# Blocks of 32 columns in place of 64 for the one-hot products of a gated mixing kernel

## The chip, the cores and the metric

The kernel runs on one core of one Trainium2 chip. The metric is the device time of one execution in microseconds; the time of a kernel is the median of its runs. The engines are TensorE (PE in the profile, its weight loads PEld), VectorE (DVE), ScalarE (ACT), GpSimd (POOL) and SyncE (SP), which here only issues transfers.

## What is computed

Two branches read the same input x of 2048 tokens by 640, and a sigmoid gate mixes them. Branch A is a Fourier mixing layer in real arithmetic. Branch B routes each token, for each of 32 heads, to two of 256 = 16 x 16 experts.

```python
a = x @ dft_hid_re.T;  b = x @ dft_hid_im.T
A = dft_seq_re @ a - dft_seq_im @ b
s1, s2 = scores of q1 with k1 and of q2 with k2      # 16 each, per token and head
# the two best of each, the two best of their four sums: expert = e1 * 16 + e2
g = softmax(the two best sums)
B = sum over heads and the two: g * gelu(x . u[expert]) * v[expert]
g0 = sigmoid(sum(x * gate_w))
out = g0 * A + (1 - g0) * B
```

For branch B the kernel never gathers rows of u and v. It computes gelu(x . u) for all 256 experts and multiplies it by a dense weight of each token and expert: the sum of the gates of the (head, choice) pairs that picked this expert. That dense weight, 16 x 16 a token, is what the changed lines compute.

## The kernel before

The order of all work is written out in the program, engine by engine; nothing is reordered later. The main loop goes over 128 sequence pieces (`seq_piece`, 4 column blocks of 512 x 16 pieces x 2 matrices). Each piece is 15 products (5 blocks of 128 by `mm3`, lines 143 to 145, three products each, since fp32 values are split in a high and a low part). Pieces are loaded five ahead (`load_piece`), and split on ScalarE and GpSimd three ahead. Behind the 128 pieces come 2 x 42 last steps (`step`), which multiply by the hidden transform and by v.

Between the products, `run_bg` lets a planner (`Pump`) put in work of branch B: every three products give it 0.68 us x 0.95 of credit, and each piece of background work, a generator, yields what it is charged. The order in which VectorE gets its work, and where TensorE turns aside for branch B, follows from these charges alone.

The scores, the two best, and the gates are made first. A transpose by DMA then gives `ROWS`, in which a partition is one (head, choice) pair (128 of them) and the columns are tokens: the first index, the second index (both as powers of two) and the gate. `experts` goes through 32 sets of 64 tokens. For each:

- `build` (line 836) makes on VectorE two tables of 128 x 1024 fp16 (lines 844 and 845): `pt` and `qt`, which hold for token and expert half e a one where the pair picked e; `pt` is then multiplied by the gate. Their columns are ordered (m, e, t): 16 groups m of four tokens t, and inside a group 16 halves e of four tokens each.
- `use` (line 848) multiplies them on TensorE, up to three sets in one visit. The sum over the 128 pairs is the contraction. One product takes the 64 columns of `pt` of one group (four tokens) as weights and the 64 columns of `qt` as the moving operand. The result is 64 x 64 for (e, t) by (f, t'); only the sixteenths with t = t' are wanted, in all a quarter. Two such blocks lie side by side in the 128 partitions of a PSUM bank.
- `mask` (line 812) clears what is not wanted: four ScalarE activations, each over the columns of one t', with a scale by partition (`mask4`) that is zero except where t = t'.
- `add_up` (line 817) sums the four columns of t' on VectorE and puts the result into `cd`, so that a partition is (block, e, t).
- `settle` (line 826) calls mask and add_up for one set each and charges 0.75 us; it runs ahead of each of the three table operations of a later set.

`store_gates` (line 793) writes `cd`, half by half, to DRAM in the order (token, e, f, m); `load_z` reads it much later for the last steps. Banks 6, 7 and 5 hold the three sets of a visit. The mask table comes from the identity matrix once (lines 342, 357 and 358). Line 380 (`w_part`) is another narrow product that the prediction compares with: 32-column weights in four blocks of partitions.

Of the kernel before, what the change touches and what calls it, by code (L numbers as in the profile page):

```python
# [8 lines left out]
F32 = mybir.dt.float32  # L9
# [3 lines left out]
AF = mybir.ActivationFunctionType  # L13
OP = mybir.AluOpType
AX = mybir.AxisListType
PSUM = bass.MemoryType.PSUM

P = 128
# [3 lines left out]
E = 16  # L22
# [12 lines left out]
GSCALE = 32768.0  # L35
# [71 lines left out]
def gated_mix_kernel(ctx: ExitStack, tc: tile.TileContext, xT, xn, dreT, dimT, wsre, wsim, wq, kT, uT, vv, gw, out):  # L107
    nc = tc.nc
    ctx.enter_context(tc.manual_schedule())

    const = ctx.enter_context(tc.tile_pool(name="const", bufs=1))
# [10 lines left out]
    def bank(n, shape=(P, TC), dt=F32):  # L122
        return psum.tile(list(shape), dt, name=f"b{n}", tag=f"b{n}")
# [4 lines left out]
    def ps_t(shape, dt=F32):  # L128
        return bank(7, shape, dt)
# [20 lines left out]
    gd = [dram.tile([2, 4, E, E, P], F32, name=f"gd{g}", tag=f"gd{g}") for g in range(2)]  # L150
# [98 lines left out]
    for q in range(2 * NC):  # L249
        n = NT * (q + 1)  # L250
# [72 lines left out]
    t = ps_t([P, TC])  # L323
    for n in range(WARM):
        c = slice(0, 2 * P) if n < WARM - 1 else slice(2 * P, TC)
# [12 lines left out]
    identf = p1.tile([P, P], F32, name="identf", tag="uf", bufs=2)  # L338
    wtab4 = const.tile([P, E, 4], F16)
    powers = const.tile([P, E], F16)  # L340
    top_bits = const.tile([P, 1], F32)
    mask4 = const.tile([P, 4], F32)

    def put_keys():
        for r in range(2):
# [6 lines left out]
    def make_tables():  # L352
        for e in range(E):
            nc.gpsimd.memset(powers[:, e:e + 1], 2.0 ** (E - 1 - e))
        nc.gpsimd.memset(top_bits, INF)
        nc.gpsimd.tensor_copy(wtab4, powers[:, :, None].to_broadcast([P, E, 4]))
        nc.vector.tensor_reduce(mask4, identf.rearrange("p (a b) -> p b a", b=4), op=OP.add, axis=AX.X)
        nc.vector.tensor_scalar(mask4, mask4, 1.0 / GSCALE, None, op0=OP.mult)

    for n, f in ((2, put_keys), (4, make_ident), (9, make_tables)):  # L360
        at(n, f)
# [124 lines left out]
    for G in range(NG):  # L486
        b = 6 + 3 * G
# [9 lines left out]
    n = b + 2  # L497
# [275 lines left out]
    for p in range(NP):  # L773
        n = N0 + 4 * p + min((p + 1) // 2, 3)
# [3 lines left out]
    for n in range(2 * NT + 3, 4 * NT + 3):  # L778
        s = n % NT
# [11 lines left out]
    summed, stored = {}, set()  # L791

    def store_gates(g):
        if g in summed and g not in stored:
            for s in range(2):
                nc.sync.dma_start(gd[g][s].rearrange("t e f m -> e t f m"), summed[g][64 * s:64 * s + 64])
            stored.add(g)

    free_sets = deque(range(4))
    HOT, used = [], []  # L800

    def experts():


        shp = [P, 16, E, 4]
        wt = wtab4[:, None].to_broadcast(shp)
        todo = deque((g, c) for g in range(2) for c in range(16))
        cd = {}

        masked, unmasked = deque(), deque()  # L810

        def mask(t):
            f = t.rearrange("p m (e t) -> p (m e) t", t=4)
            for n in range(4):
                nc.scalar.activation(f[:, :, n], f[:, :, n], AF.Copy, scale=mask4[:, n:n + 1])  # L815

        def add_up(g, c, t):
            if c == 0:
                store_gates(g - 1)
                cd[g] = p3.tile([P, E, P], F32, name="cd", tag="cd")  # L820
            nc.vector.tensor_reduce(cd[g][:, :, 8 * c:8 * c + 8].rearrange("p e m -> p m e"),
                                    t.rearrange("p m (e t) -> p m e t", e=E), op=OP.add, axis=AX.X)
            if c == 15:
                summed[g] = cd[g]

        def settle(force=False):
            us = 0.0
            if masked:
                add_up(*masked.popleft())
                us = 0.75  # L830
            if unmasked and (force or not closing):
                masked.append(unmasked.popleft())
                mask(masked[-1][2])
            return us

        def build(g, c, s):
            pt, qt = (HOT[s // 2][:, s % 2, n].rearrange("p (m e t) -> p m e t", e=E, t=4) for n in range(2))

            def row(n):
                r = ROWS[g][:, n, 8 * c:8 * c + 8, :].rearrange("p b (s t) -> p (b s) t", t=4)  # L840
                return r[:, :, None, :].to_broadcast(shp)

            assert rowed >= set(range(8 * g, 8 * g + 8))
            for o, a, b, op in ((pt, row(0), wt, OP.is_equal), (qt, row(1), wt, OP.is_equal), (pt, pt, row(2), OP.mult)):
                nc.vector.tensor_tensor(o, a, b, op=op)  # L845
                yield (0.8 if early else 1.05) + settle()

        def use(group):
            assert not last_part
            while masked or unmasked:  # L850
                yield settle(True)
            for i, (g, c, s) in enumerate(group):
                t = bank((6, 7, 5)[i], (P, 8, E * 4))
                pt, qt = (HOT[s // 2][:, s % 2, n].rearrange("p (m c) -> p m c", m=16) for n in range(2))
                for m in range(16):
                    r = slice(64 * (m % 2), 64 * (m % 2) + 64)
                    nc.tensor.matmul(t[r, m // 2, :], pt[:, m], qt[:, m], start=True, stop=True)  # L857
                unmasked.append((g, c, t))
                used.append((g, c))
                free_sets.append(s)  # L860
            yield 0.0 if todo else 4.0

        prev = []
        while todo or prev:
            group = []
            while todo and len(group) < (2 if ending else 3):
                free = [s for s in free_sets if s < 2 or not ending]
                if prev and (not free or ending and any(s > 1 for g, c, s in prev)):
                    yield from use(prev)
                    prev = []  # L870
                    continue
                if not free:
                    break
                s = min(free) if ending else free[0]
                free_sets.remove(s)
                g, c = todo.popleft()
                group.append((g, c, s))
                yield from build(g, c, s)
            if prev:
                if not group:  # L880
                    yield 2.2
                yield from use(prev)
            prev = group
        while masked or unmasked:
            yield settle(True)
# [103 lines left out]
    at(NPC - 3, make_sums, KD)  # L989
    at(NPC + 3, split_sums, KD)  # L990
    at(NPC + 14, store_gates, 1)


# [55 lines left out]
    for k, (n, m) in enumerate(((-1, 2), (0, 4), (5, 7), (7, 9), (10, 12))):  # L1049
        n, m = NT * (NC + 2) + n, NT * (NC + 2) + m  # L1050
# [19 lines left out]
    def load_z(b, n):  # L1070

        c = 2 * b + n
        bg.drain(lambda: b in summed)
        store_gates(b)
        nc.sync.dma_start(take((b, "g", n)), gdr[S + c * TC:S + (c + 1) * TC].partition_broadcast(P))
        for k in range(2):
            a, f = take((b, f"a{n + 1}{k + 1}", KD)), take((b, "zf", 2 * n + k))
            nc.sync.dma_start(a, actd[k][:, c * TC:(c + 1) * TC])
            nc.sync.dma_start(f.rearrange("p (t m) -> p t m", t=4),
                              gd[b][n].rearrange("t e f m -> (e f) t m")[k * P:(k + 1) * P])  # L1080
# [223 lines left out]
```

## Time and profile before

| | us |
|---|---|
| median of three runs | 750.85 |
| lowest and highest run | 750.09, 751.49 |
| span of the profiled execution (its total is not given apart) | 748.7 |
| TensorE matmul busy | 743.8 (99%) |
| TensorE weight loads busy | 603.8 (81%) |
| VectorE busy | 585.7 (78%) |
| ScalarE busy | 365.9 (49%) |
| GpSimd busy | 342.4 (46%) |

The span runs from the first to the last instruction of the program; the runs' time also has what lies around it. Busy time of an engine is the union of its instructions. Matmuls overlap one another, so the distance from one start to the next, not the duration, tells what one of them takes of TensorE.

### The profile page before, as it was taken

How to read it: one execution, taken by the hardware profiler on the slowest of the kernel's cores; microseconds unless marked ns; L12 is line 12 of the kernel's file. 1: busy time of each engine (PE TensorE's matmuls, PEld its weight loads, DVE VectorE, ACT ScalarE, POOL GpSimd, SP SyncE). 2: the span in 40 equal slices, each digit the busy share in tenths (PEclk: the TensorE clock that was granted, in tenths of full speed). 3: DMA queues.
4: the chain of work that ended last, by engine and by line, in shares of the span. 5: the costliest groups of instructions: out<-in, count | busy, mean ns of one | idle time of the engine just before them, and what ended most of it. 6: DMA issues, size and time to landing. Idle time of an engine off the chain costs nothing.

```text
span 748.7 us, 11141 instructions
## 1 busy us (share of the span) xinstructions
PE 743.8 (99%) x3925; PEld 603.8 (81%) x3925; DVE 585.7 (78%) x741; ACT 365.9 (49%) x664; POOL 342.4 (46%) x286
## 2 busy tenths in 40 slices
PE   9999999999999999999999999999999999999998
PEld 7777767888888888888888888888888888888887
DVE  6964098495999899999999888979899974357651
ACT  4325234543544745555463686633545653443451
POOL 5533325440532424145235456643455793487253
PEclk9999999999999999999999999999999999999999
DMA  9999999777556786972398766488876689775301
GB/s 333 392 380 364 344 374 354 231 222 250 129 176 141 190 242 157 237 200 79 114 395 285 162 168 188 133 255 280 266 234 197 222 262 343 219 239 172 113 29 71
DMA packets 84488, 171.11 MB, mean 229 GB/s; under 512 B 16080, under 2 KB 21328, under 8 KB 84176
## 3 DMA queue, kind: packets, MB, share of 16 engines
q1 hardware_dynamic: 70960, 146.13, 57.9%
q0 software_dynamic: 5472, 9.96, 8.5%
q10 hardware_dynamic: 8000, 14.31, 5.2%
q8 instruction: 31, 0.51, 0.3%
q14 instruction: 25, 0.20, 0.1%
HBM read 136.40 MB, written 32.39 MB: 225 GB/s over the span
## 4 chain that ended last, share of the span: by engine, by line
PE 94%; DMA 5%; SPq 0%; DVE 0%; ACT 0%; issue 0%; ACTq 0%
PE b L143 30%; PE b L145 30%; PE b L144 30%; PE b L239 2%; DMA wf<-in_wsre 2%; PE b L380 2%; DMA wq<-in_wq 1%; PE b L857 1%; DMA xd<-X 1%; DMA gdr<-gc 1%; DVE wp L386 0%; SPq L177 0%; ACT WS L295 0%; ACTq L514 0%; DVE ST L1191 0%
## 5 line engine op out<-in xcount | busy, mean ns | idle before, releaser
L143 PE MATMUL b<-WS,X 128*128 128x512 f32 x620 | 243.3, 392 | 0.0
L144 PE MATMUL b<-WS,X 128*128 128x512 f32 x620 | 241.4, 389 | 0.0
L145 PE MATMUL b<-WS,X 128*128 128x512 f32 x620 | 241.3, 389 | 0.0
L139 POOL TENSOR_TENSOR WS<-wf,WS 128x512 fp32r<-128x512 f32 x89 | 131.9, 1486 | 168.3 <-ACT WS L138 151.8
L143 PEld LDWEIGHTS b<-WS,X 128*128 128x128 f32 x620 | 116.3, 188 | 28.2 <-issue 4.1
L145 PEld LDWEIGHTS b<-WS,X 128*128 128x128 f32 x620 | 116.4, 188 | 24.4
L144 PEld LDWEIGHTS b<-WS,X 128*128 128x128 f32 x620 | 116.4, 188 | 23.6
L138 ACT ACTIVATE WS<-wf 128x512 fp32r<-128x512 f32 x89 | 55.5, 626 | 69.0 <-PE b L145 40.9
L845 DVE TENSOR_TENSOR hot<-rows,wtab 128x1024 f16<-128x1024 f16 x64 | 57.8, 930 | 4.3 <-PE b L857 4.3
L139 POOL TENSOR_TENSOR xl<-xf,xh 128x640 fp32r<-128x640 f32 x16 | 27.2, 1702 | 72.0 <-ACT xh L138 72.0
L567 ACT ACTIVATE sc<-b 128x512 f32<-128x512 f32 x32 | 19.9, 621 | 80.8 <-PE b L145 77.0
L191 POOL DMA_DIRECT2D WS<-in_wsre x30 | 26.4, 881 | 61.8 <-ACT WS L189 60.5
L139 POOL TENSOR_TENSOR WS<-ra,WS 128x512 fp32r<-128x512 f32 x33 | 47.1, 1439 | 14.3 <-ACT WS L138 14.1
L815 ACT ACTIVATE b<-b,mask 128x128 f32<-128x128 f32 x128 | 43.1, 342 | 14.9 <-PE b L857 11.8
L138 ACT ACTIVATE WS<-ra 128x512 fp32r<-128x512 f32 x47 | 29.4, 631 | 42.4 <-PE b L145 29.6
L622 DVE TENSOR_TENSOR eq<-sc,mm 128x1024 f16<-128x1024 f32 x32 | 44.4, 1387 | 0.9
L629 DVE TENSOR_REDUCE tied<-eq 128x64 f32<-128x1024 f16 x32 | 39.0, 1219 | 0.9
L620 DVE TENSOR_REDUCE mm<-sc 128x64 f32<-128x1024 f32 x32 | 38.7, 1211 | 0.2
L139 POOL TENSOR_TENSOR WP<-ra,WP 128x512 fp32r<-128x512 f32 x13 | 19.2, 1490 | 31.0 <-ACT WP L138 30.9
L217 DVE SCALAR_TENSOR_TENSOR ST<-ST,grow 128x512 f32<-128x512 f32 x40 | 31.7, 855 | 1.7 <-ACT tw L138 1.7
L845 DVE TENSOR_TENSOR hot<-hot,rows 128x1024 f16<-128x1024 f16 x32 | 31.6, 986 | 0.0
L143 PE MATMUL b<-WU,xh 128*128 128x512 f32 x80 | 31.1, 389 | 0.0
(209 smaller groups left out, 1449.1 us busy)
## 6 DMA issues: line engine op xcount, KB each, us to landing
X<-xd SPq DMA_DIRECT2D x36, 640.0 KB, 6.5
wq<-in_wq SPq DMA_DIRECT2D x32, 640.0 KB, 7.1
wf<-in_wsim SPq DMA_DIRECT2D x64, 256.0 KB, 4.8
wf<-in_wsre SPq DMA_DIRECT2D x63, 256.0 KB, 6.4
ra<-pd SPq DMA_DIRECT2D x40, 256.0 KB, 3.3
pd<-ST ACTq DMA_DIRECT2D x35, 256.0 KB, 5.6
WS<-in_wsre POOLq DMA_DIRECT2D x30, 256.0 KB, 6.0
xd<-X SPq DMA_DIRECT2D x11, 640.0 KB, 9.1
```

What stands on the lines that cost most here:

```text
L138: nc.scalar.activation(h, f, AF.Copy)
L139: eng.tensor_sub(l, f, h.bitcast(F32))
L143: nc.tensor.matmul(o, wh, ah, start=first, stop=False, skip_group_check=more)
L144: nc.tensor.matmul(o, wh, al, start=False, stop=False, skip_group_check=more)
L145: nc.tensor.matmul(o, wl, ah, start=False, stop=last, skip_group_check=more)
L191: nc.gpsimd.dma_start(l, (wsre, wsim)[w][c, s], accum_op=OP.add)
L217: nc.vector.scalar_tensor_tensor(f, f, -1.0 if w else 1.0, g, op0=OP.mult, op1=OP.mult)
L620: nc.vector.tensor_reduce(m, sc, op=OP.max, axis=AX.X)
L622: nc.vector.tensor_tensor(eq, sc, m[:, :, None].to_broadcast([P, HH, E]), op=OP.is_equal)
L629: nc.vector.tensor_reduce(tied[:, s, ib, :], eq, op=OP.add, axis=AX.X)
L815: nc.scalar.activation(f[:, :, n], f[:, :, n], AF.Copy, scale=mask4[:, n:n + 1])
L845: nc.vector.tensor_tensor(o, a, b, op=op)
```

## The change

Each product takes two tokens in place of four. The tables in SBUF and their order stay. A group of 64 columns (e, t) is read as c = (e, half of t) and u, the parity of t: a product takes every second column, 32 of `pt` as weights and 32 of `qt` as the moving operand. There are 32 products a set instead of 16, and four blocks of 32 partitions lie side by side in a bank, which now holds 256 columns of a set and not 512. Of each 32 x 32 block half is wanted. So `mask` is two activations of 128 elements in place of four, and `add_up` sums two columns and reads 256 elements in place of 512. `settle` charges 0.5 us in place of 0.75. The partitions of `cd` now are (block of four, e, half of t), so `store_gates` issues four DMAs of 32 partitions in place of two of 64.

```diff
-    mask4 = const.tile([P, 4], F32)
+    mask2 = const.tile([P, 2], F32)
...
-        nc.vector.tensor_reduce(mask4, identf.rearrange("p (a b) -> p b a", b=4), op=OP.add, axis=AX.X)
-        nc.vector.tensor_scalar(mask4, mask4, 1.0 / GSCALE, None, op0=OP.mult)
+        nc.vector.tensor_reduce(mask2, identf.rearrange("p (a b) -> p b a", b=2), op=OP.add, axis=AX.X)
+        nc.vector.tensor_scalar(mask2, mask2, 1.0 / GSCALE, None, op0=OP.mult)
...
     def store_gates(g):
         if g in summed and g not in stored:
-            for s in range(2):
-                nc.sync.dma_start(gd[g][s].rearrange("t e f m -> e t f m"), summed[g][64 * s:64 * s + 64])
+            for q in range(4):
+                t = gd[g][q // 2].rearrange("(t u) e f m -> u t e f m", u=2)[q % 2]
+                nc.sync.dma_start(t.rearrange("t e f m -> e t f m"), summed[g][32 * q:32 * q + 32])
             stored.add(g)
...
         def mask(t):
-            f = t.rearrange("p m (e t) -> p (m e) t", t=4)
-            for n in range(4):
-                nc.scalar.activation(f[:, :, n], f[:, :, n], AF.Copy, scale=mask4[:, n:n + 1])
+            f = t.rearrange("p m (e t) -> p (m e) t", t=2)
+            for n in range(2):
+                nc.scalar.activation(f[:, :, n], f[:, :, n], AF.Copy, scale=mask2[:, n:n + 1])
...
                 add_up(*masked.popleft())
-                us = 0.75
+                us = 0.5
...
-                t = bank((6, 7, 5)[i], (P, 8, E * 4))
-                pt, qt = (HOT[s // 2][:, s % 2, n].rearrange("p (m c) -> p m c", m=16) for n in range(2))
-                for m in range(16):
-                    r = slice(64 * (m % 2), 64 * (m % 2) + 64)
-                    nc.tensor.matmul(t[r, m // 2, :], pt[:, m], qt[:, m], start=True, stop=True)
+                t = bank((6, 7, 5)[i], (P, 8, E * 2))
+                pt, qt = (HOT[s // 2][:, s % 2, n].rearrange("p (m c u) -> p m u c", m=16, u=2) for n in range(2))
+                for q in range(32):
+                    m, u = divmod(q, 2)
+                    r = slice(32 * (q % 4), 32 * (q % 4) + 32)
+                    nc.tensor.matmul(t[r, q // 4, :], pt[:, m, u], qt[:, m, u], start=True, stop=True)
```

## Rows read from the trace of the kernel before

**Rows 1.** The page: busy us of each engine; TensorE's granted clock in 40 slices.
```profile
PE 743.8 (99%) x3925; PEld 603.8 (81%) x3925; DVE 585.7 (78%) x741; ACT 365.9 (49%) x664; POOL 342.4 (46%) x286
...
PEclk9999999999999999999999999999999999999999
```

**Rows 2.** Waits of TensorE's matmuls behind the first one: us in total, times, longest.
```profile
PE b L380 <- DMA wq<-in_wq: 0.7, 1, 0.7
```

**Rows 3.** Waits of TensorE's weight loads, same columns.
```profile
PEld L857 <- issue: 2.8, 8, 0.4
```

**Rows 4.** The page: the chain that ended last, by engine.
```profile
PE 94%; DMA 5%; SPq 0%; DVE 0%; ACT 0%; issue 0%; ACTq 0%
```

**Rows 5.** Line 857: count, duration ns min/median/max, first and last start, form.
```profile
L857 PE MATMUL b<-hot x512: 196/196/217, 419.6 to 587.6; 128*64 128x64 f16 x171
```

**Rows 6.** TensorE in time, two visits to line 857: start us, us.
```profile
445.33 0.39 PE L145 MATMUL b<-WS,X 128*128 128x512 f32 x1
445.65 0.95 PE L857 MATMUL b<-hot 128*64 128x64 f16 x48
446.53 0.50 PE L143 MATMUL b<-WS,X 128*128 128x512 f32 x1
446.87 0.39 PE L144 MATMUL b<-WS,X 128*128 128x512 f32 x1
...
587.10 0.69 PE L857 MATMUL b<-hot 128*64 128x64 f16 x32
```

**Rows 7.** TensorE in time, near the end: products of 512 and 256 columns.
```profile
739.96 0.39 PE L145 MATMUL b<-WS,ts 128*128 128x512 f32 x1
...
740.64 0.39 PE L145 MATMUL b<-WS,ts 128*128 128x512 f32 x1
...
741.46 0.28 PE L145 MATMUL b<-WP,ts 128*128 128x256 f32 x1
...
743.98 0.28 PE L145 MATMUL b<-WS,ts 128*128 128x256 f32 x1
```

**Rows 8.** Line 380: all its matmuls, and one visit in time.
```profile
L380 PE MATMUL b<-wq,kp x256: 432/432/457, 28.6 to 120.4; 128*32 128x320 f32 x128
...
40.98 0.39 PE L145 MATMUL b<-WS,X 128*128 128x512 f32 x1
41.30 2.36 PE L380 MATMUL b<-wq,kp 128*32 128x320 f32 x32
43.59 0.50 PE L143 MATMUL b<-WS,X 128*128 128x512 f32 x1
43.93 0.40 PE L144 MATMUL b<-WS,X 128*128 128x512 f32 x1
```

**Rows 9.** Groups by form: busy us, mean ns of one, idle before: tables, masks, sums, a longer reduction.
```profile
L845 DVE TENSOR_TENSOR hot<-rows,wtab 128x1024 f16<-128x1024 f16 x64 | 57.8, 930 | 4.3 <-PE b L857 4.3
...
L815 ACT ACTIVATE b<-b,mask 128x128 f32<-128x128 f32 x128 | 43.1, 342 | 14.9 <-PE b L857 11.8
...
L620 DVE TENSOR_REDUCE mm<-sc 128x64 f32<-128x1024 f32 x32 | 38.7, 1211 | 0.2
...
L821 DVE TENSOR_REDUCE cd<-b 128x128 f32<-128x512 f32 x32 | 21.7, 684 | 11.2 <-ACT b L815 10.9
```

**Rows 10.** DMA issues: store_gates' own (ns) and the pieces' landing (us).
```profile
L796 SPq DMA_DIRECT2D gd<-cd x4: 527/547/637, 487.4 to 616.8; - x4
...
wf<-in_wsim SPq DMA_DIRECT2D x64, 256.0 KB, 4.8
```

**Rows 11.** Line 380: waits that TensorE's sequencer runs by themselves.
```profile
L380 PEldq EVENT_SEMAPHORE  x14: 51/51/51, 37.1 to 116.1; - x14
```

**Rows 12.** Line 857, 445.60 to 445.86 us: what had started, duration ns, first and last start.
```profile
L857 PEld LDWEIGHTS <-hot x14: 106/113/113, 445.6 to 445.8; 128*64 128x64 f16 x14
L857 PE MATMUL b<-hot x12: 196/196/217, 445.7 to 445.8; 128*64 128x64 f16 x12
L857 PEldq EVENT_SEMAPHORE  x1: 51/51/51, 445.9 to 445.9; - x1
```

## Prediction

> **What bounds the kernel now.** I read the page's busy shares first: TensorE is busy for 743.8 of 748.7 us, and its clock is granted in full throughout [rows 1]. Busy alone does not prove that it sets the end, so the waits of TensorE come second: behind the very first, its matmuls wait 0.7 us for one transfer of weights, and nothing else is listed [rows 2]. The loads ahead of line 857 stand idle for 0.4 us in eight of its eleven visits with no releaser but "issue" [rows 3]. Line 380, the other narrow product, is entered with the same delay (below), so I read it as a fixed cost of going from 128-column products to narrower blocks, not as a wait for data. Third, the chain of work that ended last is 94% TensorE [rows 4]. So the time is the length of TensorE's instruction stream. Work on VectorE, ScalarE or a queue counts only if it makes TensorE wait, which the code around line 857 does nowhere now. What the change does to TensorE's stream counts in full.
>
> **The stream at line 857.** The 512 products go in ten visits of 48 and one of 32. A matmul of line 857 lasts 196 ns at the median [rows 5], a visit of 48 covers 0.95 us and the one of 32 covers 0.69 us [rows 6]. Durations overlap, so starts have to be compared: the 16 more matmuls, eight pairs, take 0.95 - 0.69 = 0.26 us, 32 ns a pair. Two blocks of 64 columns therefore run side by side and one turn of the two takes 32 ns.
>
> What is in these 32 ns? The price of a column comes from the last products of the kernel: matmuls of 512 columns start 0.68 / 3 = 0.227 us apart, those of 256 columns 2.52 / 21 = 0.120 us apart [rows 7]. So a column costs 0.107 us / 256 = 0.417 ns, and a product of this form has 13 ns besides. 64 columns are 26.7 ns; a turn at line 857 has some 5 ns besides. A weight load of 64 columns, one column in the same time, would be as long, and the rows can't tell which of the two a turn waits for. Both halve.
>
> **Part by part.**
>
> *Products.* 512 products of 64 columns become 1024 of 32, with 32 loaded columns each, four side by side. Turns stay 32 sets x 8 = 256: eight turns of two blocks a set become eight turns of four. If only the columns shrink, a turn goes from 32 to 32 - 32 x 0.417 = 19 ns, and 256 x 13.3 ns = 3.4 us leave TensorE's stream. That four blocks of 32 columns do run side by side is seen at line 380: its 32 matmuls of 320 columns start within 2.36 - 0.43 = 1.93 us [rows 8]; at 0.417 ns a column one behind the other would take 4.3 us. A turn of four is 0.27 us there, twice 320 columns and a few ns (these are fp32 operands, and the program gives two instructions for each matmul of line 380), so the fixed part is no larger with four blocks than with two.
>
> *Bounds of a turn of four.* The unknowns are the fixed part and the read of every second column. From below, a fixed part of nothing gives 13.3 ns, a gain of 256 x 18.7 = 4.8 us. From above, a fixed part of 13 ns as in the large products gives 27 ns, a gain of 1.3 us; and a turn that stays at 32 ns, because fp16 columns 4 bytes apart are read at half the rate, gives nothing. For the read I take full rate: the fp32 products read 4 bytes a column at 0.417 ns [rows 7], and the new columns lie 4 bytes apart. For the fixed part I take 5 ns, since both narrow forms, lines 857 and 380, show 5 ns or less.
>
> *Entry and exit.* A visit begins 0.32 us after the product before it starts, against 0.227 us otherwise, and the second product behind it comes 0.34 us after the first [rows 6]. Line 380, with 32-column blocks, shows 0.32 and 0.33 to 0.34 [rows 8]: no change. The last block's own columns and the first exposed weight load halve too; that is some 13 ns each, 11 x 0.026 = 0.3 us. Sum on TensorE: 3.4 + 0.3 = 3.7 us less.
>
> *Masks and sums.* 128 activations of 342 ns become 64 of the same 128 elements: 64 x 0.342 = 21.9 us off ScalarE. The reduction of VectorE reads 256 elements in place of 512. With 684 ns for 512 and 1211 ns for 1024, both fp32, an element costs 1.03 ns, so it becomes about 420 ns, and 32 x 0.264 = 8.4 us leave VectorE [rows 9]. Neither is in the sum: no TensorE wait names them. What hides them is TensorE's own stream; VectorE is busy 78% of the span and ScalarE 49% [rows 1], so both only get more room. From below and above: nothing to gain, since there is no stall to remove, and nothing to lose, since each operation keeps its engine and place.
>
> *The planner's price.* A sum is charged 0.5 instead of 0.75 us. Over 32 sums that is 8 us less of charge at a share of 0.95, so the stage finishes some 8.4 us earlier in TensorE's program and the last visit moves from 587 to about 579. The visits stay eleven (ten of three sets, one of two). The charge falls by 0.25 and the estimated duration by 0.26 us, so VectorE keeps the same pace against its plan. A late table of one-hot rows would show as a TensorE wait; the plan's pace gives no cause for one. Price if it does: up to the 0.93 us of one table operation [rows 9] a visit.
>
> *Stores.* store_gates issues four DMAs of 32 partitions in place of two of 64, at 0.55 us of SP each [rows 10]. So SP is held 1.1 us longer, once near 487 us and once near 617 us. Behind them stand the weight pieces, requested five pieces ahead. A piece is 15 products of 0.227 us, so that is 17 us of lead against 4.8 us of landing [rows 10]: hidden. Without this cover it would cost 1.1 us a time. The bytes are the same. The mask table is one reduction over the same 128 elements: nothing.
>
> **How this becomes a time.** The profiled span is 748.7 us, the median of the three runs 750.85; the profiled execution's own total is not given, so I carry the 2.15 us between them over as what lies around the span. 748.7 - 3.7 + 2.15 = 747.2 us.
>
> **Rivals.**
>
> *A fixed part that is not small.* If a turn of 32 columns carries the 13 ns of the large products, it takes 27 ns, and 256 x 5 ns = 1.3 us are gained: 749.6 us. For it: the large products do have 13 ns [rows 7]. Against it: the pairs show only 5. The Trainium skill has a rule that speaks for this (TensorEngine Tiling (Array Packing), section "Instruction Overhead"): a matmul has an overhead of about 60 cycles, one column takes as long as 60, and one should not tile from a dimension that is already small. By it, an estimate from its 60 cycles at 2.4 GHz, a turn would be 25 ns, the gain 1.8 us and the time 749.1 us. This trace has no product of under 64 columns, so no row shows it for one block; for single instructions it doesn't hold, as 48 of them start within 0.95 - 0.196 = 0.754 us, 16 ns each.
>
> *The turn doesn't shrink* (half-rate reads, or four fp16 blocks not side by side as two were): 32 ns, 750.5 to 750.9 us. Against it stand the four blocks of line 380 and the fp32 read rate.
>
> *Slower: the supply of instructions.* A visit of 96 products is 192 loads and matmuls, and at 19 ns a turn of eight instructions wants one every 2.4 ns; now it is four in 32 ns. What the trace shows of supply: line 380's first wait of TensorE's sequencer runs at 37.1 us [rows 11], and in program order it stands right ahead of the visit at 41.3 us [rows 8]. That is 4.2 us of products of two instructions per 0.227 us, so the sequencer leads by some 34 instructions. In the visit that begins at 445.65 us the sequencer has by 445.86 us reached a wait that stands behind 64 instructions of the visit, while 26 have started [rows 12]. Hence it gave 64 - 34 = 30 in about 0.2 us, at most 7 ns each; its lead was then 64 - 26 = 38, not smaller than before, so it may be much quicker. At 7 ns, a visit lasts (192 - 34) x 7 = 1.1 us against 0.75 now: 10.7 visits' worth x 0.35 = 3.7 us slower, 754.6. It loses from (0.75 us) / 158 = 4.8 ns an instruction on.
>
> **Chances.** My forecast, turns of 16 to 22 ns and 746.1 to 748.5 us: 0.55. The larger fixed part: 0.20. The unchanged turn: 0.10. Supply: 0.10, mostly slower. A stall that the moved plan makes: 0.05. A measurement of this kernel can tell about 0.2%, 1.5 us, from no change. So faster: 0.55 plus half of the second case and a little of the rest, 0.66; slower: supply and stall, 0.12; within: 0.22. The range takes in forecast, second case and part of the third, with the lower bound of a turn and half a us of scatter of the runs: 746.0 to 750.9 us.
>
> **What would show it.** After: as many visits to line 857, x96, each about 0.65 us from first start to last end instead of 0.95 (right); 0.8 (fixed part); 0.95 (turn unchanged); over 1.1 with loads spread evenly (supply). 64 activations of about 342 ns, reductions near 420 ns, and no new name among TensorE's waits. A named wait of TensorE in 419 to 595 us would make the part on the planner wrong; a stretch of the large products at another pace than 0.227 us would make the whole sum wrong.

## The result and the profile after

The changed kernel takes 751.67 us (median of 21 runs, 750.46 to 752.84) against 750.46 us (21 runs, 749.55 to 752.34) of the kernel before on the same chip. The medians differ by 1.21 us. The ratio, which takes in all runs, is 1.0014, with a 95% interval of 1.0009 to 1.002: 1.05 us slower, 0.7 to 1.5. The forecast was 3.7 us faster, with a range that ended at 750.9 us.

In the code after, the products are at line 859, the tables at 846, the masks at 816 and the sums at 822.

The page of the kernel after, busy shares as in [rows 1]: ScalarE has lost 22.3 us where 21.9 was forecast, and VectorE 5.6 us where 8.4 was: its sums alone are 8.3 us shorter (below), but its other work takes 2.7 us more. TensorE is still busy for 99% of the span.

```profile
span 751.1 us, 12110 instructions
PE 745.4 (99%) x4437; PEld 605.1 (81%) x4437; DVE 580.1 (77%) x741; ACT 343.6 (46%) x600; POOL 342.0 (46%) x286
```

The waits of its matmuls, as in [rows 2]; behind the very first this is the only one, and between 419 and 600 us, where the visits are, none is named:

```profile
PE b L380 <- DMA wq<-in_wq: 1.3, 1, 1.3
```

The groups of the masks and sums by form, which answer to [rows 9]:

```profile
L816 ACT ACTIVATE b<-b,mask 128x128 f32<-128x128 f32 x64 | 21.2, 343 | 17.9 <-PE b L859 16.8
...
L822 DVE TENSOR_REDUCE cd<-b 128x128 f32<-128x256 f32 x32 | 13.4, 418 | 14.7 <-ACT b L816 9.1 <-DMA gd<-cd 5.6
```

TensorE in time, five visits to line 859, to be read beside [rows 6] (start us, us):

```profile
421.25 1.09 PE L859 MATMUL b<-hot 128*32 128x32 f16 x96
...
435.42 1.07 PE L859 MATMUL b<-hot 128*32 128x32 f16 x96
...
446.17 1.08 PE L859 MATMUL b<-hot 128*32 128x32 f16 x96
...
455.96 0.39 PE L145 MATMUL b<-WS,X 128*128 128x512 f32 x1
456.28 0.97 PE L859 MATMUL b<-hot 128*32 128x32 f16 x96
457.18 0.50 PE L143 MATMUL b<-WS,X 128*128 128x512 f32 x1
...
572.28 0.68 PE L859 MATMUL b<-hot 128*32 128x32 f16 x64
```

A visit that covered 0.95 us now covers 0.97, three of them 1.07 to 1.09, and the last one 0.68 after 0.69. Seven visits are like the one at 456.28, so the eleven cover 3.24 + 7 x 0.97 + 0.68 = 10.71 us after 10 x 0.95 + 0.69 = 10.19: 0.5 us more where 3.7 less was forecast. What the visits lie between has not moved: 0.32 us from the start of the product before to the first block, as before.

The profiled spans differ by 2.4 us, more than the medians: the profiled execution of the kernel after, 752.84 us, is the slowest of its 21. Four stretches make the 2.4 us up. The first product of line 143 starts 1.0 us later (18.29 us before, 19.32 after); the wait of line 380 for weights is 1.3 us and not 0.7; the visits take 0.5; and behind the last product the program takes 0.25 us more. The first two change from execution to execution of one program: the kernel before, unchanged, started that product at 18.85 us in another execution (`e7_before_again`) and had no wait at line 380 there, and the changed kernel's repeat (`e11_after_again`) started it at 19.33 us and had none either. So the change has to answer for the visits, for the end, and for what the plan does now and then; whether it has a part in the later start is open.

The trace tells what the start hangs on. The first products of line 239, which come ahead of line 143, start some 0.43 us apart up to a certain moment and 0.23 us apart behind it. That moment is 6.5 us after the start of the span in the kernel after and 5.7 us in `e7_before_again`; in before it is 3.7 us, ahead of the first of them. The trace's record of the granted clock begins there, at 1.0. Ahead of it there is no row of the clock; the pace is the one that `e4_twice` shows at a granted clock of 0.50 (below). Products of line 239 in the first 6.5 us, in the kernel before and in the kernel after:

```profile
L239 PE MATMUL b<-WS,X x8: 389/394/499, 4.5 to 6.3; 128*128 128x512 f32 x8
...
L239 PE MATMUL b<-WS,X x4: 513/628/793, 4.8 to 6.3; 128*128 128x512 f32 x4
```

The visit at 456.28 tells why it is no shorter. Line 859 in its first 0.20 us, and then in its first 0.46 us (count, duration ns min/median/max, first and last start, form):

```profile
L859 PEld LDWEIGHTS <-hot x33: 93/93/97, 456.3 to 456.5; 128*32 128x32 f16 x33
L859 PE MATMUL b<-hot x32: 176/176/192, 456.3 to 456.5; 128*32 128x32 f16 x32
...
L859 PEld LDWEIGHTS <-hot x62: 92/93/97, 456.3 to 456.7; 128*32 128x32 f16 x62
L859 PE MATMUL b<-hot x62: 176/183/192, 456.3 to 456.7; 128*32 128x32 f16 x62
L859 PEldq EVENT_SEMAPHORE  x1: 51/51/51, 456.7 to 456.7; - x1
```

In 0.20 us 32 products have started, eight turns of four: 25 ns a turn, where 32 ns was the turn of two. Then the pace falls: the next 30 need 0.26 us, 35 ns for four. And the lead is gone, that is, the number of instructions that the sequencer has passed and that have not started yet. The sequencer's wait stands behind 128 instructions of the visit (64 loads, 64 products), and by the time it runs, 62 + 62 = 124 of them have started: the sequencer is 4 ahead. Before, it was 38 ahead at the same kind of wait [rows 12].

The third set of this visit is fast again. Line 859 in the first 0.57 and 0.74 us of the visit:

```profile
L859 PE MATMUL b<-hot x68: 176/184/192, 456.3 to 456.8; 128*32 128x32 f16 x68
...
L859 PE MATMUL b<-hot x92: 176/178/192, 456.3 to 457.0; 128*32 128x32 f16 x92
```

Behind a pause of some 0.1 us at its border, 24 products of it start in 0.17 us. Read to the ns, its turns take 25 ns but for the first and the last. In the four visits of 0.97 us that have no such pause the third set goes at 33 ns a turn instead. Either way such a visit takes 0.795 us from its first start to its last: what a pause costs, the faster turns behind it give back.

### The profile page after: what moved, and what is told of

Same layout as the page of the kernel before. It is cut to its first block, busy times and chain, and to the rows that moved or that the text cites. A ratio compares the mean times of both kernels' runs of the same rounds, so it can differ in the third digit from the quotient of the medians.

```text
span 751.1 us, 12110 instructions
## 1 busy us (share of the span) xinstructions
PE 745.4 (99%) x4437; PEld 605.1 (81%) x4437; DVE 580.1 (77%) x741; ACT 343.6 (46%) x600; POOL 342.0 (46%) x286
## 4 chain that ended last, share of the span: by engine, by line
PE 96%; DVE 2%; DMA 1%; issue 0%; ACT 0%; SPq 0%; DVEq 0%
PE b L143 30%; PE b L145 30%; PE b L144 30%; PE b L239 2%; PE b L380 2%; PE b L859 1%; DMA wq<-in_wq 1%; DVE ST L217 1%; PE b L326 1%; DVE tw L139 0%; DVE WU L139 0%; DVE wp L386 0%; DVE tt L409 0%; ACT WU L138 0%; DVE tt L412 0%
## 5 line engine op out<-in xcount | busy, mean ns | idle before, releaser
L846 DVE TENSOR_TENSOR hot<-rows,wtab 128x1024 f16<-128x1024 f16 x64 | 55.9, 898 | 3.2 <-PE b L859 3.2
L217 DVE SCALAR_TENSOR_TENSOR ST<-ST,grow 128x512 f32<-128x512 f32 x40 | 33.3, 888 | 2.3 <-DMA grow<-gdr 1.6
L143 PE MATMUL b<-WU,xh 128*128 128x512 f32 x80 | 31.1, 389 | 0.0
L144 PE MATMUL b<-WU,xh 128*128 128x512 f32 x80 | 31.1, 389 | 0.0
```

The costliest lines, as they stand in the source:

```text
L143: nc.tensor.matmul(o, wh, ah, start=first, stop=False, skip_group_check=more)
L144: nc.tensor.matmul(o, wh, al, start=False, stop=False, skip_group_check=more)
L217: nc.vector.scalar_tensor_tensor(f, f, -1.0 if w else 1.0, g, op0=OP.mult, op1=OP.mult)
```

## Experiments

Theories at the start, for the gain that isn't there. A: a turn of four has a floor of 25 ns, and after the first set TensorE takes instructions as fast as its sequencer delivers them. B: the sets after the first are slower for what they touch, their bank or their tables.

**`e1_one_set`: one set a visit.**

```diff
             for i, (g, c, s) in enumerate(group):
...
                 free_sets.append(s)
+                if i < len(group) - 1:
+                    yield 0.7
+            bg.credit += 0.7 * (len(group) - 1)
```

The visit now gives way after each set but the last, so that three products of the main loop come between two sets; the last line gives the planner its credit back.

> The changed kernel, but a visit to the products holds one set (32 products, 64 loads and matmuls) instead of three, so there are 32 visits instead of 11. Theory A (TensorE's sequencer supplies an instruction every 4.2 ns and lives on a lead of some 34; a turn of four blocks takes 25 ns while the lead lasts, 33 ns after): 64 instructions never use up the lead, so every visit runs at 25 ns a turn, first to last start about 0.20 us, busy 0.38 us each. Stream 32 x 0.20 = 6.5 us against 8.8; 21 more entries and exits of 0.31 us add 6.5 us; sum 4.2 us longer than the changed kernel, about 755.5 to 756. Theory B (turns of the second and third set are slow because of what ScalarE and VectorE do in the banks and tables meanwhile, or because of the tables they read): two thirds of the visits stay at 33 ns a turn, 0.27 us from first to last start, busy 0.45 us.

756.36 us, ratio 1.0078 (1.0048 to 1.0107). What had been one visit of 96, TensorE in time:

```profile
456.58 0.38 PE L859 MATMUL b<-hot 128*32 128x32 f16 x32
456.89 0.50 PE L143 MATMUL b<-WS,X 128*128 128x512 f32 x1
457.23 0.40 PE L144 MATMUL b<-WS,X 128*128 128x512 f32 x1
457.46 0.40 PE L145 MATMUL b<-WS,X 128*128 128x512 f32 x1
457.79 0.38 PE L859 MATMUL b<-hot 128*32 128x32 f16 x32
...
458.99 0.38 PE L859 MATMUL b<-hot 128*32 128x32 f16 x32
```

All 32 products of a set now start within 0.38 - 0.18 = 0.20 us, in the second and third set too, with the banks and tables they had. B falls. 32 sets of 0.20 us are 6.4 us, less than the 8.0 us that the sets took before (10 x 0.752 + 0.50), but 21 more visits, each with its way in and out, cost more than that.

**`e2_adjacent`: the same products on columns that lie side by side** instead of every second one.

```diff
-"p (m c u) -> p m u c"
+"p (m u c) -> p m u c"
```

> The changed kernel with 32 adjacent columns in place of every second one; this pairs the wrong tokens, the work is the same. Theory A: no difference, turns of 25 ns in the first set and 33 ns after, a visit of 96 covers 0.97 us. Theory C (columns 4 bytes apart cost reading time): turns go to 19 ns in the first set, a visit covers 0.80 us or less.

751.48 us in one run; turns of 25 and then 33 ns as with every second column, and most visits of 0.97 us. The stride costs nothing.

**`e3_sixteen`: the same loads, but only 16 moving columns**, and with them half of a set's columns in the bank and one mask activation a set.

```diff
-                    nc.tensor.matmul(t[r, q // 4, :], pt[:, m, u], qt[:, m, u], start=True, stop=True)
+                    nc.tensor.matmul(t[r, q // 4, :], pt[:, m, u], qt[:, m, u, :16], start=True, stop=True)
```

> The changed kernel with only 16 of the 32 moving columns of each product (half of the experts' second index is left out, with one mask activation a set). If a turn is 12 ns and 0.417 ns a column, the first set runs at 18 ns a turn, 0.15 us from first to last start. If 25 ns is a floor that columns don't move, it stays at 25 ns, 0.20 us. Theory A: from the second set on 33 ns either way, a visit of 96 still covers 0.95 us or more, since the supply of instructions and not the columns sets it.

751.74 us in one run. A visit of it in time:

```profile
465.84 0.96 PE L859 MATMUL b<-hot 128*32 128x16 f16 x96
```

Line 859 in the first 0.21 us of this visit:

```profile
L859 PEld LDWEIGHTS <-hot x33: 93/94/98, 465.8 to 466.0; 128*32 128x32 f16 x33
L859 PE MATMUL b<-hot x32: 168/169/186, 465.8 to 466.0; 128*32 128x16 f16 x32
```

With half of the moving columns, the first set still takes 0.20 us (32 products) and the visit 0.96 us in place of 0.97. So moving columns set neither pace here. The loads still have 32 columns; that these alone make the 25 ns isn't excluded by this run.

**`e4_twice`: each turn of four issued twice**, so that a set has 128 instructions of the same kind, in the same bank, behind the same waits.

```diff
-                for q in range(32):
+                for q in [4 * k + i for k in range(8) for _ in range(2) for i in range(4)]:
```

> The changed kernel with every group of four products issued twice into the same place (192 products a visit, the result is the same). Theory A: after the lead is gone, the added 96 products take 8 x 4.2 = 33 ns a turn: 0.8 us a visit more, 10.7 visits' worth 8.5 us, about 760. The first set no longer runs through at 25 ns: the lead of 34 ends inside it, after some 136 instructions at the latest. Theory B would keep its whole first set, now 128 instructions, at 25 ns a turn.

782.82 us (ratio 1.043, 1.039 to 1.047): far more than expected. Two things lie in it. The pace falls from 25 to 33 ns after some 64 instructions, now in the middle of the first set: it goes by the count of instructions since the visit began, not by sets. A visit of 192 that nothing disturbed covers 1.78 us, first to last start 1.60; one of 96 has 0.97 - 0.18 = 0.79. The 96 more products, 24 turns, take 0.81 us: 34 ns a turn of eight instructions, 4.2 ns each, the lasting rate.

```profile
508.80 1.78 PE L859 MATMUL b<-hot 128*32 128x32 f16 x192
```

The rest was not in the expectation. Its first part is pauses. Six visits are broken by a pause in which TensorE waits for nothing that the profile names ("issue", in brackets), 2.1 to 3.8 us from one start to the next. TensorE in time, one of them:

```profile
447.45 1.68 PE L859 MATMUL b<-hot 128*32 128x32 f16 x144
451.09 0.53 PE L859 MATMUL b<-hot 128*32 128x32 f16 x48 [1.96 <-issue]
```

The page, the queue of instruction transfers (packets, MB, share):

```profile
q8 instruction: 43, 0.70, 0.4%
```

A seventh pause, 1.8 us of idle time, stands at line 145 just behind a visit. Counted in TensorE's stream, the seven lie some 512 or 1024 instructions apart, and each ends 1.2 to 1.6 us after a transfer on the instruction queue has ended (43 of them, 0.70 MB / 43 = 16 KB each; the kernel after has 35). I take this to mean that the sequencer ran out of fetched instructions, some 18 us in all; no row names it. The second part is the clock, in two stretches (start:end and length in us, PE busy and its products, granted clock, DMA share, GB/s):

```profile
466.94:470.35 3.41, 3.41 (x10) 0.50 0.00 0
535.21:542.03 6.82, 6.21 (x17) 0.50 0.38 135
```

A granted clock of 0.50 is the lower of the two levels, 1.2 in place of 2.4 GHz; the products of 512 columns then start 0.43 us apart in place of 0.227. The two stretches stand at the two longest pauses, of 3.1 and 3.6 us of idle time (the first begins 1.6 us behind its pause, the second inside its own), and over 10.2 us they cost about 5 us. The kernel after shows no such pauses, and its granted clock is 1.0 from 6.5 us up to the last half microsecond of the span, so both are costs of this experiment and not of the change.

One thing in this trace speaks against a simple form of A. Behind four of the six pauses in visits the turns go at 25 ns again; in the visit at 447.45 us six turns do, and then the pace falls to 33 ns, just as behind the start of a visit. A sequencer that had just run out of instructions should have no lead to give. A limit behind TensorE that also goes by the count of instructions and recovers in any pause would give the same paces; against it speaks the lead of 4 in place of 38. No run separates the two.

**The half microsecond that the visits don't explain.** Three candidates: the smaller charge of a sum lets the tables come late (the planner), the two added stores (four of 32 partitions), or an unseen price of the new products. `e5_before_charge50` puts the charge alone into the kernel before, `e8_before_four_stores` the stores alone; `e6_after_charge75` and `e9_after_two_stores` take either out of the kernel after.

The edit of e5, on the kernel before; e6 is its reverse on the kernel after:

```diff
-                us = 0.75
+                us = 0.5
```

> The kernel before with only the planner's charge of a sum changed, 0.5 in place of 0.75 us; products, masks and sums as before. Theory A: the charge moves visits, and TensorE waits for none of what moves, so 0.0 us against before, within 0.3. Theory P (part of the millisecond's 1.05 us that the change lost comes from the places that the planner now gives the work): about 0.5 us longer. The last visit should come some 8 us earlier than 587 us.

> The changed kernel with the old charge of 0.75 us a sum. Theory A: as the changed kernel, 0.5 to 1.0 us longer than before, since the stream of a visit is the same: 0.795 us from first to last start in most visits. Theory P: it falls back to 0.5 us or less above before.

`e5_before_charge50`: 751.53 us, ratio 1.0014 (1.0005 to 1.0023). The charge alone costs as much as the whole change, with the old products, masks and sums. Its profile names the place. Waits of TensorE's matmuls:

```profile
PE b L857 <- DVE hot L845: 0.9, 1, 0.9
```

The same place in time, TensorE and VectorE:

```profile
512.08 0.69 PE L857 MATMUL b<-hot 128*64 128x64 f16 x32
...
512.96 0.68 DVE L845 TENSOR_TENSOR hot<-hot,rows 128x1024 f16<-128x1024 f16 x1
...
513.69 0.44 PE L857 MATMUL b<-hot 128*64 128x64 f16 x16 [0.92 <-DVE hot L845]
```

The third set's table is finished inside the visit, and TensorE stands for it. `e6_after_charge75`: 751.68 us, ratio 1.0022 (1.0012 to 1.0032; one of its eleven runs took 755.02 us), with no wait of TensorE's matmuls between 419 and 600 us and the last visit back at 587.4 us. The charge matters, but the changed kernel isn't saved by the old one: by its trace (visits 0.34 us, end 0.25) e6 should be 0.6 us slower, below its interval of 0.9 to 2.4.

`e7_before_again` is the kernel before, unchanged.

> The kernel before once more, for a second trace: how far the start (first product of the main loop) and the wait for the weights of line 380 scatter from one execution to the next. The changed kernel's profiled execution had 1.0 us more at the start and 0.6 us more at line 380 than the first trace of before. If that is scatter, this trace lies between them or beyond; if the changed program really starts later, it lies within 0.2 us of the first trace.

The repeat of the kernel before, 750.09 us in one run: all visits as in [rows 6], the start 0.55 us later and no wait at line 380. So both change between executions of one program.

The edit of e8, on the kernel before:

```diff
-            for s in range(2):
-                nc.sync.dma_start(gd[g][s].rearrange("t e f m -> e t f m"), summed[g][64 * s:64 * s + 64])
+            for q in range(4):
+                t = gd[g][q // 2].rearrange("t e f m -> e t f m")[8 * (q % 2):8 * (q % 2) + 8]
+                nc.sync.dma_start(t, summed[g][32 * q:32 * q + 32])
```

e9, on the kernel after:

```diff
-            for q in range(4):
-                t = gd[g][q // 2].rearrange("(t u) e f m -> u t e f m", u=2)[q % 2]
-                nc.sync.dma_start(t.rearrange("t e f m -> e t f m"), summed[g][32 * q:32 * q + 32])
+            for s in range(2):
+                t = gd[g][s].rearrange("(t u) e f m -> u e t (f m)", u=2)
+                nc.sync.dma_start(t, summed[g][64 * s:64 * s + 64].rearrange("p f m -> p (f m)"))
```

> The kernel before with only the stores of the changed kernel: four transfers of 32 partitions in place of two of 64. Theory S (the added transfers shift the round of eight transfer semaphores, so that SyncE's wait for the very last transfer stands earlier among the waits that end the program, and six waits instead of two follow it at 0.06 us each): the stretch from the last product's start to the end grows from 3.60 to 3.85 us, the visits stay 0.75 us, and the time grows by 0.25 us. Rival (the end is later because the program of TensorE is longer): 3.60 us, no change.

> The changed kernel with two transfers of 64 partitions a store, as before. Theory S: the stretch at the end is 3.60 us again; what is left against before is the visits, 0.3 to 0.6 us longer in all, so 0.3 to 0.6 us above before and 0.25 us under the changed kernel. Rival: 3.85 us at the end and 0.6 to 1.1 us above before.

Both say what the stores cost: nothing where they run, 0.25 us at the end of the program. SP's wait for the last output at the end (us in total, times, longest), in the kernel before:

```profile
SPq L1300 <- DMA out_y<-ST: 1.0, 1, 1.0
```

In the kernel after:

```profile
SPq L1302 <- DMA out_y<-ST: 1.3, 1, 1.3
```

In e8, the old products with four stores:

```profile
SPq L1301 <- DMA out_y<-ST: 1.3, 1, 1.3
```

In e9, the new products with two:

```profile
SPq L1302 <- DMA out_y<-ST: 1.0, 1, 1.0
```

From the start of TensorE's drain of 2345 ns to the end of the span it is 748.7 - 743.0 = 5.7 us before and 749.4 - 743.7 = 5.7 in e9, but 751.1 - 745.2 = 5.9 after and 748.3 - 742.4 = 5.9 in e8. Read to the ns, from the start of the last product to the end of the program, it is 3.60 us in the profiles of all five kernels with two stores (before, e5, e7, e9, e10) and 3.84 to 3.86 us in those of seven with four (after, e1, e2, e3, e6, e8, e11); e4, which has four too, shows 3.90. The drains, of before:

```profile
L1300 PEldq DRAIN  x2: 13/1179/2345, 743.0 to 748.2; - x2
```

Of after:

```profile
L1302 PEldq DRAIN  x2: 13/1179/2345, 745.2 to 750.6; - x2
```

At the end SP waits for eight semaphores of transfers one after the other, about 0.06 us each when they have long been met. The program gives them to transfers in turn, so that two more transfers twice shift the turn: the wait for the very last transfer now comes with six waits behind it, before with two. The whole time of `e8_before_four_stores`, 750.62 us (ratio 1.0004, 0.9995 to 1.0013), is compatible with that 0.25 us and with nothing. `e9_after_two_stores`: 751.6 us, ratio 1.0016 (1.0007 to 1.0025). Its profile has a late table in the kernel with the new products; TensorE in time:

```profile
511.70 0.68 PE L859 MATMUL b<-hot 128*32 128x32 f16 x64
512.96 0.38 PE L859 MATMUL b<-hot 128*32 128x32 f16 x32 [0.57 <-DVE hot L846]
```

**`e10_after_mended`** has the charge of 0.75 and the two stores of e9 in the kernel after; **`e11_after_again`** is the kernel after beside it.

The edits are those of e6 and e9 together.

> The changed kernel with the old charge of 0.75 us and with two transfers a store. If the loss is the sum of the visits (0.3 to 0.5 us, supply of instructions), the end (0.25 us) and now and then a table that comes late because the plan is tight (up to 0.7 us), this kernel keeps only the visits: 0.3 to 0.5 us above before, an end of 3.60 us, no wait of TensorE for a table, tables of the third sets 2 us ahead or more but for the first visit.

> The changed kernel once more beside the mended one. By the same sum 0.6 to 1.5 us above before, an end of 3.85 us, tables of the third sets in part under 1 us ahead, in some executions a wait of TensorE for a table inside a visit; so 0.3 to 1.0 us above the mended kernel.

751.21 us (ratio 1.0014, 1.0005 to 1.0023) and 751.75 us (1.0015, 1.0005 to 1.0025). e10's profile has no wait for a table, and its end is 3.60 us; still it isn't measurably faster than e11, and it is slower than before. What is left in it are the products and a wait. The products: visits that sum to 8.75 us from first to last start where the kernel before has 8.02, less some 0.2 us because the product behind a visit follows its last block 20 ns sooner. The wait is for a piece of weights; the profile of e11 has the same one, with 0.4 us, and none of the other eleven has it:

```profile
PE b L144 <- DMA WS<-in_wsim: 0.3, 1, 0.3
```

The two were run side by side, so whether the change has a part in this wait isn't shown.

## Why the prediction was wrong

**The step that failed is the turn of four** (*Products* and *Bounds of a turn of four*). I split the 32 ns of a pair into 26.7 ns of columns and 5 ns besides, and let the first halve. The sum 256 x 13.3 ns rests on a turn of 19 ns; the first sets show 25 ns, and e3 shows that fewer moving columns leave it there. A slope between 512 and 256 columns tells what a column costs where columns set the pace; it doesn't tell that they still do at 32. The rival with the larger fixed part was near: 27 ns by the large products. That the 25 ns belong to the turn and not to each of its eight instructions is suggested by their spacing: the four products of a turn start within 10 ns, and 15 ns pass to the next turn. At 25 ns throughout, 256 x 6.7 = 1.7 us would still have been gained. The Trainium skill (TensorEngine Tiling (Array Packing), "Instruction Overhead") gives each matmul an overhead of about 60 cycles, which by an estimate is 25 ns at 2.4 GHz. The trace agrees with that page for a turn of four, at 32 and at 16 columns; for a single product it doesn't, since four of them start in one turn.

**That gain went to a pace of 4.2 ns an instruction**, which I read as the supply of instructions, the rival I gave 0.10 and priced at up to 7 ns an instruction. The price is 4.2 ns (`e4_twice`), and by my own working it should have been a gain still, since I put the break-even at 4.8. That working gave the lead of 34 instructions away free: (192 - 34) x 4.2 = 0.66 us. But the first 64 instructions take 0.20 us whatever the lead, and the other 128 then cost 128 x 4.2 = 0.53: with the 0.06 us or so that go at the last set's border it is 0.79, as measured, against 0.75 before. The pace doubled in instructions: four in 32 ns were 8 ns each, well over 4.2, and eight in 25 ns are 3.1, under it. What is measured is the pace, the even spacing of loads and products (one of each about every 8 ns), the count after which it starts and the lead of 4 in place of 38. That the sequencer is the place is argued from these and not shown; no row names it. Why the lead of 34 to 38 is used up after some 64 instructions, when 3.1 against 4.2 ns would take some 130, I can't count out, and the fast turns behind the pauses of e4 don't fit a spent lead.

**Three visits are another 0.1 us longer** (1.07 to 1.09). At the border of the second and third set a turn takes 55 ns, or 107 where the sequencer runs a wait of 51 ns; beyond that, single pauses of some 0.1 us are in these visits. The second visit has one in all seven profiles with visits of 96 products, and of the four with the old products only e5 has any, where tables are late. Their cause stays open.

**Entry and exit**: right. 0.32 us into a visit, and the product behind it comes 20 ns sooner, 11 x 0.02 = 0.2 us in place of the 0.3 I gave.

**Masks and sums**: right in size (343 ns x 64, 418 ns x 32, where 342 and 420 were forecast) and right that they pay nothing.

**The planner's price**: right in the direction and in the eleven visits, wrong in size and in its conclusion. From the first visit to the last it is 151.0 us after and 167.5 before, 16.4 us less where 8.4 was forecast, and 15.6 less in e5; why it is twice as much is open. I reasoned that VectorE keeps its pace, because charge and duration fall alike. But its sums got only 8.3 us shorter, and tables that come just in time have a margin, and mine was never read. From the end of a third set's last table to the first product that uses it there are 0.77 us in the first visit before and 0.75 after. In the others it is 1.4 us at the least before and 0.58 after; in e5 and, once, in e9 it falls to under 0.06 us, which is no margin. The price I had put beside it, up to 0.93 us a visit, is about what the two showed (0.9 and 0.6). In the profile of the kernel after no table is late; how often one is over its runs, I can't say.

**Stores**: right where they run, blind at the end of the program, where they cost 0.25 us.

**From the span to the time**: I carried 2.15 us over as what lies around the span. In each run on record it is 1.7 to 1.9 us; the 0.4 us between came from setting a median beside the span of one execution.

The sum: visits 0.3 to 0.6 us, by the profiles with the new products; the end 0.25; and a late table of 0.6 us now and then. That gives 0.55 to 1.45 us, and 1.05 (0.7 to 1.5) was measured. It doesn't close for e6, whose 0.6 us lie below what was measured. For e10 the visits' 0.5 us lie inside its interval of 0.4 to 1.7 us, but like e6 it has no late table in its profile and was not measurably faster than the changed kernel. One candidate is the start: the first product of line 143 begins between 18.29 and 18.85 us in four profiles of kernels with the old products, and between 18.27 and 19.33 us in nine with the new ones, on the mean 0.46 us later. By the trace that is how long TensorE runs its first products at the lower pace: up to 3.7 to 5.7 us after the start of the span in the four, up to 4.0 to 6.7 us in the nine. The two overlap, the code there is the same, and the kernel before alone shows 3.7 and 5.7 us, so scatter is likely; no run tells it from a cause.

No kernel here beats the one before. Visits of one set have the faster turn and pay 21 more ways in and out. Longer visits, four sets, were not tried: they want four tables ready at once, and it is the third that comes late now.

## What to carry over

Before a narrow product is cut into more, narrower ones, count instructions and not columns: find what a turn costs in the narrowest blocks seen, take that as a floor, and set the instructions of a visit against the pace that a long run of them keeps, with only the first few dozen faster. A charge in a plan that is lowered along with the work it stands for can still eat the margin of whatever is just in time; read that margin in the trace (end of the producer to start of the consumer) before calling the move neutral. A change that adds transfers should be followed to the waits at the end of the program.

## What the runs showed of the hardware

- A turn of four 32-column blocks side by side takes 25 ns with 32 moving columns and 25 ns with 16; two blocks of 64 columns took 32 ns.
- A long run of these weight loads and products goes at 4.2 ns an instruction. About the first 64 instructions of a visit go faster (3.1 ns), and so do up to as many behind a pause.
- TensorE's first products run at half pace up to 3.7 to 6.7 us after the start of the span, and that moment differs between executions of one kernel (3.7 and 5.7 us); the first product of line 143 starts between 18.3 and 19.3 us accordingly.
- Reading every second fp16 column costs nothing against adjacent ones (0.97 us a visit in either).
- Visits of 384 instructions stalled six times for 2.1 to 3.8 us, each time until 1.2 to 1.6 us behind the end of a 16 KB transfer of the instruction queue; visits of 192 showed none of this size. At the two longest stalls the granted clock fell to 0.5 for 3.4 and 6.8 us.
- SyncE waits for eight semaphores of transfers in turn at the end; which of them the last transfer has makes 0.25 us of difference here.
